# Keeping two row blocks on chip, pairing the row work and ordering the weight gradients by hand in an adaLN block's backward kernel

## The chip, the cores and the metric

One core of a Trainium2 chip. The metric is the device time of one execution in microseconds (us), median over the runs of a kernel. A comparison of times below uses fast runs only, and unless said otherwise of kernels that ran on the same chip in the same rounds. Single profiles are compared by stretch, with the granted clock beside them (1.00 is full speed of TensorE's clock). PE is TensorE, DVE VectorE, ACT ScalarE, POOL GpSimd; SP issues the transfers, SPq is its queue. "Fill" is matmul work without a fixed place, put where TensorE would wait.

## The reference

```python
def _fwd(A_x, A_w_r, A_w_i, B_w1, B_b1, B_w2, B_b2, c, w_mod):   # S=2048, D=512, F=1792, bf16
    sa, ca, ga, sb, cb, gb = (silu(c) @ w_mod) in six rows of 512
    h = layernorm(x) * (1 + ca) + sa
    x = x + ga * irfft2(rfft2(h) * (w_r + 1j * w_i))           # spectral branch
    h = layernorm(x) * (1 + cb) + sb
    x = x + gb * (relu(h @ w1 + b1) ** 2 @ w2 + b2)            # squared-ReLU MLP
    return x
_out, _vjp = jax.vjp(_fwd, ...); _grads = _vjp(grad_out)       # ... the output and nine gradients
```

## The kernel before

Transforms are GEMMs. The order of work: generated tables and the forward spectral stages (the gradient of h, `gT x w2T`, fills TensorE's holes: its 512-column results are evicted to `gab`), the forward rows, the FFN in four blocks of four rows, backward spectral stages, backward rows, with the gradients of w1 and w2 as fill. A scheduler orders each engine's instructions by priority; `LATE` means "only if nothing else is ready". The parts that the change touches:

```python
def rstd(nc, dst, var, K):                                    # GpSimd, two instructions
    nc.gpsimd.tensor_scalar(dst, var, 1e-5, None, op0=ALU.add)
    nc.gpsimd.tensor_tensor(dst, dst, K["nhalf"][...], op=ALU.pow)

def stage_g(b):                                               # forward rows, one at a time
    ...
        psY = spec_g23(tc, K, CS, t, rows, psR, psR)          # 4 psT matmuls, Tsb on ACT, 1 psY matmul
        nc.scalar.copy(out=yb[:, j, :], in_=psY)
        nc.vector.tensor_tensor(yg, yb[:, j, :], modb[:, GA_B, :], op=ALU.mult)
        nc.vector.tensor_tensor(xb[:, j, :], yg, xb[:, j, :], op=ALU.add)
        nc.vector.bn_stats(st, xb[:, j, :]); nc.vector.bn_aggr(mv, st)
        rstd(nc, inv2[:, t:t + 1], mv[:, 1:2], K)
        nc.vector.tensor_scalar(n2rows[:, hf + j, :], xb[:, j, :], mv[:, 0:1], inv2[:, t:t + 1], ...)
        nc.gpsimd.tensor_tensor(xb[:, j, :], xb[:, j, :], gbb2, op=ALU.add)      # bias b2
    nc.sync.dma_start(y_dram[...], yb); ...; nc.sync.dma_start(x1_dram[...], xb)
    ...
# backward spectral stages: all loads first, stores when a step is done
for gi in range(8):
    ...LF, Z (w_r), Z (w_i), X of group gi are loaded; n2_sb after gi == 1...
nc.sync.dma_start(K["LG"], LG_dram); nc.sync.dma_start(K["LGx"], LGx_dram)
def ew_b(gi, G):
    cmul(nc, ew, Z[gi], G, ...)
    gW = ew.tile([P, 2, 2, FP], BF16, name="gW")              # two buffers
    cmul(nc, ew, Xt[gi], G, gW...)
    nc.sync.dma_start(out2_view[...], gW...); nc.sync.dma_start(out3_view[...], gW...)
with Priority(tc, LATE):
    ...for fb in range(NFB): grad_w1(fb)                      # 16 units of 16 matmuls, then w2's 14
```

The order of the FFN stages g, t, h, o, gn of the four blocks is the same in both kernels.

## Time and profile before

The median was 585.62 us of 3 runs (583.81 to 588.2) when the prediction was made. The stretches of the profiled run (579.1 us), cut where TensorE starts another kind of work; the first inverse transform is the short one with `psG` matmuls:

| stretch | begins with | us | PE idle, us |
|---|---|---|---|
| start | launch | 98.6 | not used |
| inverse transform | first psG | 14.2 | 0 |
| C, forward rows | end of psG | 55.5 | 10.2 |
| D, FFN | first hidden-layer matmul | 189.5 | 18.2 |
| E, backward | first backward psB | 221.3 | 37.7 |

A stretch tells more than the whole: PE is busy 84% of the span, but C, E's first 54 us and the end lose for three different reasons. The lines themselves are in the prediction.

### The profile page before, as it was taken

What the parts mean: (1) busy time and instruction counts of PE and PEld (TensorE: products, weight loads), DVE (VectorE), ACT (ScalarE), POOL (GpSimd) and SP (SyncE); (2) the same over time, 40 slices, a digit from 0 to 9 for tenths busy, and PEclk for the clock granted to TensorE, in tenths of its full rate; (3) what the DMA queues carried; (4) which work ended last, traced back from release to release, by engine and by line L of the source; (5) the groups of instructions that cost most, each with busy time, mean ns of one, the idle gap of its engine ahead of it and who ended that gap; (6) DMA issues with size and microseconds to landing.
All of it is one profiled execution on the core that took longest, in us unless ns stands there. A gap on an engine that the chain in (4) does not pass through costs nothing. (4 is left out here: it accounts for less than half of the span.)

```text
span 579.1 us, 8005 instructions
## 1 busy us (share of the span) xinstructions
PE 486.9 (84%) x2670; PEld 239.3 (41%) x2710; DVE 386.6 (67%) x1016; ACT 241.8 (42%) x418; POOL 51.9 (9%) x130
## 2 busy tenths in 40 slices
PE   1767999987889898997889969895799978977977
PEld 0523467833334343443444423462563333433423
DVE  6897978378739679388348545362987999564531
ACT  3656754354535234243252412560267633244210
POOL 4233000046200004004000000000000000000000
PEclk9989999999999998999989989798899997999989
DMA  8958723467449329955954997897559953249991
GB/s 289 250 214 234 254 64 86 161 191 218 164 127 291 128 80 274 247 200 163 241 171 152 257 191 162 274 249 229 113 138 283 234 161 102 65 120 258 255 230 52
DMA packets 157409, 109.64 MB, mean 189 GB/s; under 512 B 87090, under 2 KB 144312, under 8 KB 156600
## 3 DMA queue, kind: packets, MB, share of 16 engines
q1 hardware_dynamic: 157368, 109.13, 68.0%
q8 instruction: 21, 0.34, 0.2%
q14 instruction: 20, 0.16, 0.1%
HBM read 43.22 MB, written 45.44 MB: 153 GB/s over the span
## 5 line engine op out<-in xcount | busy, mean ns | idle before, releaser
L646 PE MATMUL mm<-gT,w2T 128*128 128x512 bf16 x218 | 54.7, 379 | 16.2 <-DVE gab L649 10.5
L838 PE MATMUL og<-w,h 128*128 128x512 bf16 x219 | 55.9, 399 | 2.8 <-DVE h L781 1.8
L773 PE MATMUL mm<-h2T,w 128*128 128x512 bf16 x216 | 53.9, 386 | 2.4 <-ACT r L775 1.5
L1004 PE MATMUL mm<-g_sb,hn 128*128 128x512 bf16 x219 | 51.0, 388 | 3.9 <-DVE gw L1007 2.9
L775 ACT ACTIVATE r<-mm,b1col 128x512 bf16<-128x512 f32 x56 | 38.3, 688 | 38.0 <-PE mm L773 18.9
L941 PE MATMUL mm<-gab,n_sb 128*128 128x448 bf16 x256 | 53.1, 361 | 1.1 <-ACT gb1bc L934 0.6
L810 PE MATMUL og<-w1T,gab 128*128 128x512 bf16 x220 | 49.8, 379 | 0.3
L646 PEld LDWEIGHTS <-w2T 128*128 128x128 bf16 x224 | 21.5, 97 | 45.6 <-issue 16.7
L941 PEld LDWEIGHTS <-n_sb 128*128 128x128 bf16 x256 | 24.9, 99 | 27.3 <-issue 6.5
L1004 PEld LDWEIGHTS <-hn 128*128 128x128 bf16 x224 | 21.8, 99 | 32.4 <-issue 8.4
L773 PEld LDWEIGHTS <-w 128*128 128x128 bf16 x224 | 21.2, 98 | 32.9 <-issue 14.0
L838 PEld LDWEIGHTS <-h 128*128 128x128 bf16 x224 | 21.7, 102 | 28.3 <-issue 4.8
L394 PE MATMUL psT<-Cf,utcs 128*128 128x512 bf16 x123 | 32.5, 379 | 0.2
L810 PEld LDWEIGHTS <-gab 128*128 128x128 bf16 x224 | 21.5, 98 | 26.2 <-issue 1.5
L777 DVE TENSOR_TENSOR gab<-r,gab 128x512 bf16<-128x512 bf16 x56 | 27.1, 483 | 7.7 <-ACT r L775 7.1
L458 DVE SCALAR_TENSOR_TENSOR gm_junk<-wmc,onef,gmbc 128x512 bf16<-128x512 bf16 x24 | 18.0, 750 | 19.0 <-DMA wmc<-in_w_mod_dram 18.6
L812 ACT ACTIVATE cb<-og,inv 128x512 bf16<-128x512 f32 x16 | 10.9, 686 | 45.3 <-PE og L810 29.2
L742 POOL TENSOR_TENSOR xb<-xb,gbb 128x512 bf16<-128x512 bf16 x16 | 19.4, 1215 | 106.0 <-DVE n2rows L741 106.0
L649 DVE CAST gab<-mm 128x512 bf16<-128x512 f32 x28 | 19.2, 686 | 13.0 <-PE mm L646 13.0
L379 PEld LDWEIGHTS <-Z 128*128 128x128 bf16 x256 | 25.1, 98 | 6.3 <-DVE gW L415 1.7
L341 PE MATMUL psC<-AE,LFb 128*128 128x257 bf16 x120 | 17.1, 297 | 8.7 <-ACT G L343 8.6
L781 DVE TENSOR_TENSOR h<-r 128x512 bf16<-128x512 bf16 x56 | 23.2, 415 | 0.0
(282 smaller groups left out, 851.8 us busy)
## 6 DMA issues: line engine op xcount, KB each, us to landing
gh_dram<-gab SPq DMA_DIRECT2D x28, 256.0 KB, 3.2
h_dram<-h SPq DMA_DIRECT2D x28, 256.0 KB, 2.9
w<-in_B_w_dram SPq DMA_DIRECT2D x2, 1792.0 KB
wm<-in_w_mod_dram SPq DMA_DIRECT2D x3, 1024.0 KB, 11.7
wmc<-in_w_mod_dram SPq DMA_DIRECT2D x6, 512.0 KB, 5.3
out_dram<-gwm SPq DMA_DIRECT2D x6, 512.0 KB, 4.4
Z<-in_A_w_r_dram SPq DMA_DIRECT2D x16, 128.5 KB, 3.0
Z<-in_A_w_i_dram SPq DMA_DIRECT2D x16, 128.5 KB, 5.0
```

The lines of the kernel that those rows point to most:

```text
L379: nc.tensor.matmul(ps[:, ch, :], lhsT=Z[gi][:, x, ri, f0:f0 + P], rhs=lg_window(K, g, e + ri), start=(n == 0), stop=(n == 3))
L394: nc.tensor.matmul(ps, lhsT=CS[:, t, c].rearrange("p r a b -> p (r a b)"), rhs=K["Cf"][:, c, :], start=(c == 0), stop=(c == 3))
L646: nc.tensor.matmul(ps, lhsT=w2T[:, dc, fc * P:(fc + 1) * P], rhs=gT[b][:, dc, :], start=(dc == 0), stop=(dc == 3))
L742: nc.gpsimd.tensor_tensor(xb[:, j, :], xb[:, j, :], gbb2, op=ALU.add)
L773: nc.tensor.matmul(ps, lhsT=w1[:, dc, fc * P:(fc + 1) * P], rhs=h2T[b][:, dc, :], start=(dc == 0), stop=(dc == 3))
L775: nc.scalar.activation(r, ps, AF.Relu, bias=b1col[:, fc:fc + 1])
L777: nc.vector.tensor_tensor(gh, r, gh, op=ALU.mult)
L781: nc.vector.tensor_tensor(hT[b, fc], r, r, op=ALU.mult)
L810: nc.tensor.matmul(ps, lhsT=gaT[b][:, fc, j * P:(j + 1) * P], rhs=w1T[:, fc, :], start=(fc == 0), stop=(fc == NFC - 1))
L838: nc.tensor.matmul(ps, lhsT=hT[b, fc][:, j * P:(j + 1) * P], rhs=w2[:, fc, :], start=(fc == 0), stop=(fc == NFC - 1))
L941: nc.tensor.matmul(ps[:, 0:W4], lhsT=n2_sb[:, t, dc * P:(dc + 1) * P], rhs=ghn[t // 4][:, t % 4, fs], start=(t == 0), stop=(t == NT - 1))
L1004: nc.tensor.matmul(ps, lhsT=hn[:, t, :], rhs=g_sb[:, t, :], start=(t == 0), stop=(t == NT - 1))
```

## The change

Its intent: take the statistics' chain off GpSimd, halve the number of small row instructions, save 8 MB of round trips, and place each gradient GEMM by hand where another engine or a transfer would leave TensorE idle. The core of the diff (cuts marked):

```diff
+def rstd_act(nc, dst, var, K):
+    nc.scalar.activation(dst, var, AF.Sqrt, bias=K["eps"])
+    nc.vector.reciprocal(dst, dst)
 ...
+    AEs = make_ae(nc, lfp)            # was inside spec_f23: zeroed padding column of the AE tiles
 ...
-                nc.sync.dma_start(y_dram[:, ts, :], yb)
-                nc.sync.dma_start(x1_dram[:, ts, :], xb)
+            x1b[b] = rows.tile([P, TB, D], BF16, name="x1")
+            yb[b] = rows.tile([P, TB, D], BF16, name="y")
+            for j in range(0, TB, 2):            # pairs of rows
+                nc.vector.tensor_tensor(yg, y, modb[:, GA_B, None, :].broadcast_to([P, 2, D]), op=ALU.mult)
 ...
+                rstd_act(nc, inv2[:, t:t + 2], mv[:, :, 1], K)
-                    nc.gpsimd.tensor_tensor(xb[:, j, :], xb[:, j, :], gbb2, op=ALU.add)
 ... stage_o
+                    nc.tensor.matmul(ps, lhsT=K["ones_sq"][0:1, :], rhs=b2row, start=True, stop=False)
 ... backward spectral stages
-        for gi in range(8): ...all loads...
+        for gi in range(2):
+            load(gi)
-            gW = ew.tile([P, 2, 2, FP], BF16, name="gW")
+            gW = ew.tile([P, 2, 2, FP], BF16, name="gW", bufs=3)
+        def after_b(gi):
+            if gi + 2 < 8:
+                load(gi + 2)
+            if gi == 5: ...LG, LGx...
+            if gi > 0:
+                fill_w1(2)
-    with Priority(tc, LATE): ...grad_w1, grad_w2...
 ... last loop, per pair of rows
+            fill(t // 2)                          # one w1 or w2 unit
 ... GMod.emit: wmc and gwm in halves with bufs=4 instead of one whole buffer each
```

## The prediction

> **What bounds the kernel now.** I read the page's head first, then the busy time of each engine in eight stretches cut at the borders that the TensorE timeline shows, then TensorE's list of waits in the stretches with gaps, then the VectorE and TensorE timelines inside two of them. The head and the slices of the page:
>
> ```profile
> span 579.1 us, 8005 instructions
> PE 486.9 (84%) x2670; PEld 239.3 (41%) x2710; DVE 386.6 (67%) x1016; ACT 241.8 (42%) x418; POOL 51.9 (9%) x130
> PE   1767999987889898997889969895799978977977
> ```
>
> TensorE (PE) is the only engine near full. Its gaps lie in the first eighth, the fourth eighth and the last third. The stretches (columns: stretch, length, busy time of PE, weight load, DVE, ACT, POOL, granted clock, DMA share, GB/s):
>
> ```profile
> 113.50:167.00 53.50, 44.01 (x242) 19.72 (x245) 35.61 (x75) 26.11 (x47) 18.34 (x28) 1.00 0.52 163
> 167.00:357.00 190.00, 171.11 (x833) 74.53 (x849) 122.55 (x313) 69.35 (x108) 14.73 (x20) 0.96 0.73 200
> 357.00:411.00 54.00, 40.88 (x239) 23.69 (x241) 27.33 (x56) 19.11 (x36) 0.14 (x2) 0.84 0.82 232
> 428.00:511.00 83.00, 75.05 (x386) 32.25 (x387) 66.64 (x202) 39.78 (x83) 0.00 (x0) 0.96 0.59 167
> 511.00:579.00 68.00, 53.59 (x234) 22.80 (x238) 28.78 (x70) 18.73 (x32) 0.00 (x0) 0.97 0.80 191
> ```
>
> Call them C (forward row stage: x1, statistics, n2, filled with the first weight GEMM), D (the FFN), E1 (backward spectral stages), E2 (backward rows with the w1 gradient as fill) and E3 (w2 gradient alone). PE is idle 9.5 us in C, 19 in D, 13 in E1, 8 in E2, 14 in E3. TensorE's waits in C and in E1 name the two largest:
>
> ```profile
> PE mm L646 <- DVE gab L649: 9.0, 6, 2.6
> ...
> PE psC L341 <- ACT G L343: 8.6, 1, 8.6
> PE mm L930 <- DMA LFb<-LF_dram: 3.7, 1, 3.7
> ```
>
> In C, VectorE is late with an eviction because it sits, in order, behind rows whose rstd comes from GpSimd (VectorE timeline):
>
> ```profile
> 132.10 0.41 DVE L741 TENSOR_SCALAR n2rows<-xb,l_mv,inv 128x512 bf16<-128x512 bf16 x1 [0.77 <-POOL inv L405]
> 132.43 0.69 DVE L737 BATCH_NORM_STATS2 l_st<-xb 128x6 f32<-128x512 bf16 x1
> 133.03 1.00 DVE L734 TENSOR_TENSOR yg<-yb,modb 128x512 bf16<-128x512 bf16 x1
> 133.95 0.17 DVE L739 BATCH_NORM_AGGREGATE l_mv<-l_st 128x2 f32<-128x6 f32 x1
> 134.06 0.43 DVE L735 TENSOR_TENSOR xb<-yg,xb 128x512 bf16<-128x512 bf16 x1
> 134.41 0.68 DVE L649 CAST gab<-mm 128x512 bf16<-128x512 f32 x1
> ```
>
> The reader is to see 0.77 us waited for GpSimd, and yg taking 1.00 us where it takes 0.42 elsewhere: GpSimd runs its x1+bias add (1.15 us) just then. The n2 writes start at 132.1, 135.2, 138.4, 141.5: 3.15 us a row. TensorE needs 1.95 us a row (psY starts at 129.6 and 131.6 where nothing waits). In E1 the 8.6 us gap is a transfer: the chain of waits has an output store of the weight gradient gW taking 10.70 us at 390.8, queued behind bulk loads; gW has two buffers, VectorE stops, then ACT, then PE. In E3 the chain of waits alternates between w2-gradient matmuls, gwm stores and 5 us loads of wmc, which has one buffer.
>
> [...] tensor_tensor in bf16 takes 0.42 us on 512 columns and 0.69 on 1028, so a pair saves 0.15 us. [...] Both loads of this trace take 1283 ns; the changed kernel has a third, at its first Sqrt, and none later. [...] after the 8.6 us gap, 16 psC matmuls took 3.60 us against 1.95, and E1's granted clock is 0.84.
>
> **The change, part by part.** A built version gives the instruction order per engine; what follows uses it.
>
> *Start, 0 to 98.6.* Nearly untouched. The small AE memset moves ahead of the iotas that delayed it (a 2.2 us PE wait), and the order interleaves the first spectral groups earlier. Gain 3 us, between 0 and 8, a choice.
>
> *C.* Out go the GpSimd rstd (0.36 + 0.57 us a row), its bias add and the 0.42-to-1.00 stretching; in come a Sqrt on ACT and a reciprocal, per pair. VectorE per pair of rows was 6.3 us; now 2 x 0.69 (yg, x1), 2 x 0.69 (statistics), 2 x 0.18, 2 x 0.41 (n2), some 0.7 for Sqrt and reciprocal, one eviction of 0.69: 5.3 us against PE's 3.9. Also, since x1, y and n2 are held as two blocks of four, only 9 psY rows and 12 psT groups come before the FFN instead of 16; the last 66 GEMM matmuls (14 us) hide the rows. PE work at the pace of 0.216 us for 512 columns (56 w2-gradient matmuls in 12.48 us give 0.22): 114 x 0.216 + 48 x 0.216 + 9 x 0.216 + 1.5 = 38.4 us. With 3 us of stalls C is 41.5 instead of 53.5: gain 12.
>
> *D.* It receives the moved work, 16 psT + 7 psY = 5.0 us, and 16 new matmuls for the b2 row, 16 x 0.216 = 3.5 us. Pairing takes some 11 us off VectorE in the two products of the hidden layer (27.1 + 23.2 us in 112 instructions, about 39 in 56) and 5 in the row products; but VectorE is busy 64% here and not the bound. The y and x1 round trips through DRAM go (4 x 2 MB of 109.6 MB): they are hidden, only 2.5 us of PE waits in D name any load. Of the waits on n2rows, h, gx and gp (4.2 + 1.8 + 4.2 + 1.0) I let 3 us go; the n2 chain of the third block now has little filler after its last psY. Net loss 5.5 us.
>
> *E, 357 to 579, 222 us.* PE work by the paces of the timeline: spectral 13.8 + 13.9 + 13.7, w1 gradient 256 x 0.189 = 48.4, its bias sums 6, rows 17.3 + 5.1, w2 gradient 48.4: 166.7 us; over the mean granted clock of 0.96, 173.5. So 48 us is loss. Now two w1 units (6 us of PE) follow each spectral step: PE per step 10 us, VectorE 4 x 0.69 + 4 x 0.42 (4.0) + 2 x 2.0 = 8, so PE stays the bound; gW has three buffers, bulk LG loads come late, the next step's loads are spread. The 8.6 us gap and the slow clock behind it should go. In the row loop one GEMM unit per pair gives PE 6.3 us against VectorE's 4.5. In the tail wmc and gwm have four buffers. What stays: some 4 us at the start while Z and the 2 MB n2 load land (PE has 16 us of work before the first w1 unit); 3 us where n1 rows queue behind g (2 MB) and four transposed loads that cannot start before the LG space is free; 4 us in the tail; 3.5 us last eviction and store; 7 us of short gaps. 173.5 + 21.5 = 195: gain 27.
>
> Sum: 3 + 12 - 5.5 + 27 = 36.5 us, some 6%; 585.6 - 36.5 = 549, and I say 548.
>
> **Rivals.** (a) *A wait takes the place of the one removed*: TensorE's order is now fixed by hand, so a late load stops everything: the first w1 unit waits for n2, the first w2 units for g and hn, the rows for n1. For: n_sb took 10.6 us to land, hn 6.5, and the order puts four hn loads and g ahead of n1. Against: 12 to 16 us of PE work stands before each. With 6 to 8 us at each place, 565. (b) *VectorE becomes the bound* in the interleaved spectral steps: 8 of 10 us is close, and in-order gradient evictions sit inside the complex products. For: VectorE was busy 16.96 of 17 us at 411 to 428. It would cost about 1.5 us a step: 560. (c) *The transfers were hidden, and the x1/y part gives nothing*: this I believe of the DRAM part by itself; if the ACT Sqrt also just replaces the GpSimd wait, C gains only 5 us: 555. (d) *The gaps and the clock go together*: if E reaches 185 us and the clock stays near 1, 535.
>
> **Range and chances.** All rivals but a double failure leave more than 2% (under 574). PE work over the clock, plus the unavoidable start and end, is about 505, so under 525 is unlikely. Range 530 to 567. Faster by over 2%: 0.93; within: 0.05; slower: 0.02.
>
> **What would show it.** Right: PE's wait on gab gone from C, GpSimd near 20 us busy in all, the first hidden-layer matmul at about 150 us instead of 168; no gap over 3 us in the backward spectral steps, w1-gradient matmuls inside them and a clock above 0.95 there; DMA near 101 MB; the part from the first backward spectral matmul to the end near 195 us. Wrong: PE waits on n_sb, hn, g_sb or n1 of 5 us and more; VectorE above 90% in E1; ACT waiting for statistics before a Sqrt while Tsb is late; D longer than 200 us.

"Both loads of this trace" are the two table loads of ScalarE, at 0.73 and 10.66 us. The paces are the trace's: eight psB matmuls of 512 columns take 1.89 us with 0.38 for a single one, so (1.89 - 0.38) / 7 = 0.216 us each; thirteen of 448 columns take 2.62 with 0.35 for one, so 0.189. No trace stood behind the 0.7 us for Sqrt and reciprocal: that was the author's estimate. In the changed kernel it is 0.66 us from the end of the statistics (128.30) to the end of the reciprocal (128.96).

## The result, and the profile after

The changed kernel took 544.93 us (median of 4, 540.11 to 545.98) against 584.71 (median of 4, 578.83 to 588.2): the ratio is 0.9335, 95% interval 0.9236 to 0.9434. A ratio is the mean time of one kernel's fast runs over that of the other's fast runs of the same rounds, so not quite the ratio of the quoted medians. The prediction of 548 was 3 us off, in its range, and on the side it favoured.

The head and the slices of the page of the kernel after, to be held against those of before:

```profile
span 542.6 us, 7664 instructions
PE 483.9 (89%) x2684; PEld 237.9 (44%) x2726; DVE 362.5 (67%) x872; ACT 245.3 (45%) x427; POOL 16.5 (3%) x88
PE   0779899999987999999789997988999999789995
```

PE does the same work (483.9 against 486.9 us busy) in a span 36.5 us shorter. GpSimd fell from 51.9 to 16.5 us, VectorE by 24. The stretches C, D, E's spectral part, its rows and its end (columns as in the prediction: PE, weight load, DVE, ACT, POOL, clock, DMA share, GB/s):

```profile
108.30:150.40 42.10, 40.63 (x234) 18.72 (x238) 24.84 (x53) 21.84 (x40) 0.00 (x0) 1.00 0.24 77
150.40:347.10 196.70, 180.65 (x861) 78.05 (x876) 113.01 (x232) 78.28 (x125) 0.14 (x2) 0.95 0.66 178
347.10:424.40 77.30, 72.49 (x459) 39.47 (x462) 55.78 (x126) 27.70 (x51) 0.00 (x0) 0.98 0.70 207
445.40:511.00 65.60, 59.73 (x265) 23.88 (x269) 45.58 (x112) 37.96 (x77) 0.00 (x0) 0.95 0.98 253
511.00:542.60 31.60, 24.82 (x113) 10.27 (x112) 23.05 (x60) 10.91 (x21) 0.00 (x0) 0.96 0.90 240
```

C is all but full (1.5 us idle). D has 16 us idle and a clock of 0.95. In the rows the transfer engines are busy 98% of the time. VectorE's order in C, where before it waited 0.77 us for GpSimd in every second row and 0.17 us in the others:

```profile
126.16 0.73 DVE L748 TENSOR_SCALAR n2rows<-x,l_mv,inv 128x512 bf16<-128x512 bf16 x2
126.80 1.28 DVE L744 BATCH_NORM_STATS2 l_st<-x 128x6 f32<-128x512 bf16 x2
128.00 0.30 DVE L745 BATCH_NORM_AGGREGATE l_mv<-l_st 128x2 f32<-128x6 f32 x2
128.21 0.67 DVE L739 TENSOR_TENSOR yg<-y,modb 128x1024 bf16<-128x1024 bf16 x1
128.80 0.16 DVE L413 RECIPROCAL inv<-inv 128x2 f32<-128x2 f32 x1
128.91 0.69 DVE L740 TENSOR_TENSOR x<-yg,x 128x1024 bf16<-128x1024 bf16 x1
129.52 0.68 DVE L651 CAST gab<-mm 128x512 bf16<-128x512 f32 x1
130.12 0.73 DVE L748 TENSOR_SCALAR n2rows<-x,l_mv,inv 128x512 bf16<-128x512 bf16 x2
```

No line has a wait in brackets; the n2 writes of two pairs stand 3.96 us apart, where two single rows took 6.3. The next pair's yg is placed between one pair's statistics and its reciprocal, so the Sqrt's latency is covered: it runs on ScalarE from 128.33 to 128.62 us, and this reciprocal starts at 128.80. Of the four reciprocals in C the first and the last waited for it, 0.94 and 0.36 us.

| stretch | before | after | gain | predicted |
|---|---|---|---|---|
| start | 98.6 | 94.2 | 4.4 | 3 |
| inverse transform | 14.2 | 14.1 | 0.1 | 0 |
| C | 55.5 | 42.1 | 13.4 | 12 |
| D | 189.5 | 196.7 | -7.2 | -5.5 |
| E | 221.3 | 195.5 | 25.8 | 27 |
| span | 579.1 | 542.6 | 36.5 | 36.5 |

That the sum fits to the digit is luck: by medians the gain is 39.8 us, and the profile before is of the fastest run. Other profiles with the old code in E took longer there (b_nobias 223.5 us, b_ae 224.6, x_front 228.1; b_rstd's 230.7 is of a slow run), so against them E gained 28 to 33 us; those with the old start have their first psG at 98.9 to 101.0 us instead of 98.6. D, 187.4 to 190.7 us in all profiles with the old code there, does not depend on the choice. A sum that fits this well can also hide terms that are wrong in their reason. Twelve runs looked for them.

### The profile page after: what moved, and what is told of

The parts are those of the page before. It is cut to its first block, busy times and chain, and to the rows that moved or that the text cites. A ratio compares the mean times of both kernels' runs of the same rounds, so it can differ in the third digit from the quotient of the medians.

```text
span 542.6 us, 7664 instructions
## 1 busy us (share of the span) xinstructions
PE 483.9 (89%) x2684; PEld 237.9 (44%) x2726; DVE 362.5 (67%) x872; ACT 245.3 (45%) x427; POOL 16.5 (3%) x88
## 2 busy tenths in 40 slices
DMA packets 142094, 101.11 MB, mean 186 GB/s; under 512 B 86242, under 2 KB 129000, under 8 KB 141288
## 3 DMA queue, kind: packets, MB, share of 16 engines
HBM read 38.90 MB, written 41.25 MB: 148 GB/s over the span
## 5 line engine op out<-in xcount | busy, mean ns | idle before, releaser
L839 PE MATMUL og<-w,h 128*128 128x512 bf16 x218 | 57.5, 407 | 3.7 <-DVE h L784 2.9
L944 PE MATMUL mm<-gab,n_sb 128*128 128x448 bf16 x256 | 51.9, 361 | 3.1 <-DMA n_sb<-n_dram 3.1
L817 DVE SCALAR_TENSOR_TENSOR jk<-cb,onef,n2rows 128x512 bf16<-128x512 bf16 x16 | 12.0, 749 | 28.0 <-ACT cb L814 28.0
L400 ACT ACTIVATE Tsb<-psT 128x512 bf16<-128x512 f32 x32 | 19.0, 596 | 23.4 <-PE psT L397 23.0
L651 DVE CAST gab<-mm 128x512 bf16<-128x512 f32 x28 | 19.2, 685 | 14.2 <-PE mm L648 14.2
L782 DVE TENSOR_TENSOR gab<-r,gab 128x1024 bf16<-128x1024 bf16 x28 | 19.3, 689 | 10.6 <-ACT r L780 10.6
L840 ACT CAST o<-og 128x512 bf16<-128x512 f32 x16 | 9.2, 587 | 34.6 <-PE og L839 34.6
L653 ACT CAST gab<-mm 128x512 bf16<-128x512 f32 x28 | 16.3, 581 | 15.6 <-PE mm L648 15.6
```

Source lines behind the costliest of these rows:

```text
L651: nc.vector.tensor_copy(out=gaT[b][:, fc, :], in_=ps)
L782: nc.vector.tensor_tensor(gh, r, gh, op=ALU.mult)
L839: nc.tensor.matmul(ps, lhsT=hT[b, fc][:, (j + i) * P:(j + i + 1) * P], rhs=w2[:, fc, :], start=False, stop=(fc == NFC - 1))
L944: nc.tensor.matmul(ps[:, 0:W4], lhsT=n2_sb[:, t, dc * P:(dc + 1) * P], rhs=ghn[t // 4][:, t % 4, fs], start=(t == 0), stop=(t == NT - 1))
```

## The experiments

"First psB to second psG" below is the stretch in which the backward spectral steps run, up to the inverse transform.

### 1 and 2. The two halves: x_front and x_tail

The kernel is cut at the end of the FFN. x_front is the changed code before the cut and the old code after it; x_tail is the other way round (only names and the shape of one row adapted, and the X store padded, as the other half needs).

> The changed kernel up to the end of the FFN, the old code from the backward spectral stages to the end. Theory (the two halves add up, E is worth 26 us and the front 10): 585 - 10 = 575 us, ratio to before 0.983. Rival 1 (the front sets up the tail: early ghn loads, n2 stored whole, so part of E's gain comes with the front): 565 or less, ratio 0.966. Rival 2 (the front is worth nothing in time because the old tail waits for the same loads): 584, ratio 1.00.

> The old code up to the end of the FFN, the changed code from the backward spectral stages to the end. Theory: 585 - 26 = 559 us, ratio 0.956; no PE gap over 4 us in the spectral steps. Rival 1 (part of E's gain needs the front): 568 or more, ratio 0.97. Together with the other hybrid the two gains should add up to the whole change's 40 us within 6.

Measured on one chip with before at 587.57: x_front 573.1 (ratio 0.9751, interval 0.9686 to 0.9815), x_tail 557.46 (0.9488, 0.9421 to 0.9556). The gains are 14.5 and 30.1 us, 44.6 together where the whole change gave 39.8 by its medians: they add up within the 6 us asked for, so neither half needs the other within that error. In x_tail the first hidden-layer matmul still comes at 170 us and the stretch from first psB to second psG is 78.4 us, as in the changed kernel. In x_front the old gap is there again (PE waits 11.3 us for G). So two thirds of the change are behind the FFN.

### 3 and 4. The forward rows: b_rstd and b_nobias

Both are the kernel before with one of the two things that left GpSimd.

```diff
 b_rstd
-  rstd(nc, inv2[:, t:t + 1], mv[:, 1:2], K)
+  rstd_act(nc, inv2[:, t:t + 1], mv[:, 1:2], K)
 b_nobias
-  nc.gpsimd.tensor_tensor(xb[:, j, :], xb[:, j, :], gbb2, op=ALU.add)      (and the making of gbb2)
+  nc.tensor.matmul(ps, lhsT=K["ones_sq"][0:1, :], rhs=b2row, start=True, stop=False)   (stage_o)
```

> Kernel before with one edit: rstd of the second layernorm by a Sqrt on ScalarE and a reciprocal on VectorE, row by row; the x1+bias add stays on GpSimd, the rows stay single. Theory (VectorE's in-order wait for GpSimd's rstd makes evictions late): the 9.0 us of PE waits on gab in the forward row stage fall below 4, total 579 us, ratio 0.99. Rival 1 [...]: waits stay at 7 to 9 us, ratio 1.00. Rival 2 (ScalarE becomes late with Tsb, which is the same stall by another name): waits on Tsb of 4 us and more take their place.

> Kernel before with one edit: the GpSimd add of the bias to x1 goes, the bias enters stage o by a K=1 matmul as in the changed kernel; rstd stays on GpSimd. Theory (the add only stretches VectorE a little: 16 x 0.6 us of yg): waits on gab fall by 2 of 9 us, 16 new matmuls cost 3.5 us in the FFN, total 586 us, ratio 1.00. Rival [...]: waits on gab fall below 3 us, yg takes 0.42 us, and total 581 us, ratio 0.993.

What the runs show is the stretching itself, yg at 1.00 us beside GpSimd's add and 0.42 without, and the rivals are that this makes VectorE late.

PE's waits in C of b_rstd, then VectorE's waits in C of b_nobias (columns: engine, instruction, what it waited for, us in total, times, longest):

```profile
PE psY L399 <- ACT Tsb L397: 3.6, 5, 1.5
PE pst L760 <- DVE h2T L763: 0.6, 1, 0.6
```

```profile
DVE gab L646 <- PE mm L643: 7.8, 9, 1.1
DVE n2rows L740 <- POOL inv L405: 6.3, 8, 0.9
```

With Sqrt on ScalarE the 9.0 us of waits on gab are 0.5, and waits of 3.6 us on Tsb come up: ScalarE, now in the chain, is late in five places. C falls from 55.5 to 50.9 us. With the bias add gone and rstd still on GpSimd, VectorE waits for rstd as before (6.3 us in 8 rows, 5.7 before) and PE on gab 6.3 us; C stays at 55.4 us, as 2.4 us more of the fill GEMM fell into it (PE busy 47.7 instead of 45.3). yg, which took up to 1.00 us before, takes 0.39 to 0.43 in all 16 rows, so GpSimd's add did stretch it (by what mechanism was not shown). The theories hold: without the in-order wait for rstd 8.5 of the 9.0 us go, without the bias add 2.7; the two shares overlap. In times, b_rstd cannot be judged: three of its four runs counted as slow (583.9 us median, the one fast run 574.0), the profiled one among them; the granted clock in C was 1.00 all the same, as in the kernel before. Of the remaining 8.8 us between 50.9 and the changed kernel's 42.1, 4.9 are moved work (PE is busy 40.6 us in C instead of 45.5, since two blocks of four rows need only 9 psY before the FFN) and 3.3 the waits on Tsb, of which 0.3 us are left there.

b_nobias took less time all the same, 577.8 us, ratio 0.9836 (0.9768 to 0.9905; whether it is more than 2% is unclear), which no theory had. Its trace shows most of it in the start: the first psG came at 91.2 us instead of 98.6. The edit was not clean: with GpSimd's order changed, the zeroing of the AE tiles (their padding column) stood at 12.22 us, in the kernel before at 57.15. That led to the next experiment.

### 5. The start: b_ae

GpSimd's order in the kernel before, and the TensorE matmul that waits for its last line; then the same two in the changed kernel (columns: start, length, engine and line, operation, tiles, in brackets the idle time before it and what ended it):

```profile
56.65 0.55 POOL L138 IOTA cf_dr<- 128x512 int32 x1
57.15 0.14 POOL L332 MEMSET AE<- 128x2 bf16 x2
57.31 0.60 PE L341 MATMUL psC<-AE,LF 128*128 128x257 bf16 x4 [2.21 <-POOL AE L332]
```

```profile
1.30 0.14 POOL L327 MEMSET AE<- 128x2 bf16 x2
40.57 0.27 PE L343 MATMUL psC<-AE,LF 128*128 128x257 bf16 x1
```

A zeroing of 0.14 us stands behind every table that GpSimd generates, and these wait for VectorE (6.77 us before 53.47, 5.67 before 41.16). The page counts 2.2 us of PE waiting, because PE spent some 12 us before it on fill. b_ae is the kernel before with only this moved:

```diff
-        AEs = [aep.tile([P, 2, 514], BF16, name=f"AE{i}") for i in range(2)]     (in spec_f23)
-        for ae in AEs: nc.gpsimd.memset(ae[:, :, 256:257], 0.0)
+    AEs = make_ae(nc, lfp)                                                       (first thing, and from cdp for the way back)
```

> Kernel before with one edit: the AE tiles of the forward and backward spectral stages are allocated and their padding column zeroed early, as in the changed kernel, so that the zeroing no longer stands at the end of GpSimd's order. Theory (the start's gain comes from this alone): the first forward psC starts near 41 us instead of 57, the first psG at 91 to 94 instead of 98.6, the wait of 2.2 us on GpSimd is gone, total 5 us under before, ratio 0.991. Rival (PE only does its fill GEMM later): first psG earlier but the forward row stage longer by the same amount, ratio 1.00.

Ratio 0.9874 (0.9822 to 0.9926), 582.72 against 589.29. The first psC now starts at 41.25 us, the first psG at 92.9, but C grew to 59.0, because more fill was left for it (PE is busy 51.1 us there instead of 45.3): the first hidden-layer matmul comes 2.2 us earlier and the first backward psB 2.9. So theory and rival are both half right: some 5.7 us were gained at the start and 3.5 given back in C. The rest of the measured 6.6 us is not explained; that the profile before is of a fast run will be part of it.

### 6, 7 and 8. The gap in the backward spectral stages: b_gw3, b_lglate, b_loads

The prediction said that the 8.6 us gap was a store queued behind bulk loads, with gW's two buffers too few. The kernel before with each of the changed kernel's three remedies alone:

```diff
 b_gw3
+            gW = ew.tile([P, 2, 2, FP], BF16, name="gW", bufs=3)
 b_lglate
         spec_f23(..., ew_b)
+        nc.sync.dma_start(K["LG"], LG_dram); nc.sync.dma_start(K["LGx"], LGx_dram)      (were ahead of it)
 b_loads
-        for gi in range(8): ...loads...
+        for gi in range(2): load(gi)
+            if gi + 2 < 8: load(gi + 2)                  (in ew_b, after the two stores; LG at gi == 5)
```

> Kernel before with one edit: the tile gW of the backward spectral stages gets three buffers instead of two. Theory (the 8.6 us gap comes from VectorE waiting for a gW buffer whose store is queued behind bulk loads): the gap on G falls below 2 us, the stretch from the first backward psB to the second psG falls from 54 to about 46 us, total 8 us under before, ratio 0.986. Rival (the queue of transfers is the limit, not the buffer): a gap of 5 us or more appears at the next load or the next store, the stretch stays above 51 us, ratio 1.00.

> Kernel before with one edit: the two bulk loads of the inverse transform's tables (LG, LGx) are issued after the spectral loop instead of before it; two gW buffers stay. Theory (the store that held the gap waited behind these loads): the gap on G falls below 3 us, the stretch falls to about 47 us, and psG waits for LG under 2 us; ratio 0.986. Rival 1: psG waits 4 us and more for LG, ratio 1.00. Rival 2: the gap stays because Z, LF and X loads are queued there too, ratio 1.00.

> Kernel before with one edit: in the backward spectral stages only two groups are loaded ahead, each further group's loads are issued after the step's gW stores, LG at step 5, as in the changed kernel; two gW buffers stay. Theory (the single in-order transfer queue held the first gW store behind the loads of all eight groups, so neither a third buffer nor moving LG alone helped): first gW store issued within 3 us of its data instead of 12, gap on G under 3 us, the stretch from first psB to second psG 46 us instead of 54, total 8 us under before, ratio 0.986. Rival (bandwidth: 232 GB/s in that stretch is all there is): gaps of 5 us and more at loads, stretch above 51 us, ratio 1.00.

None of them was shown to be faster: ratios 1.0043 (0.9979 to 1.0106), 0.999 (0.9842 to 1.0139) and 1.0032 (0.9962 to 1.0102). The stretch from first psB to second psG took 52.1, 54.3 and 56.8 us, against 54.1. In b_gw3 VectorE's wait for a gW buffer was still 14.4 us (15.7 before) and PE's gap, 9.7 us, had only moved on to the first psG. The transfer queue of the kernel before shows why a third buffer changes little (all of these are issued by SP, one after the other):

```profile
387.38 1.72 SPq L962 DMA_DIRECT2D Z<-in_A_w_i_dram  x1
389.15 0.47 SPq L967 DMA_DIRECT2D LGb<-LG_dram  x1
389.66 0.43 SPq L968 DMA_DIRECT2D LGxb<-LGx_dram  x1
390.13 0.62 SPq L974 DMA_DIRECT2D out_dram<-gW  x1
390.80 0.76 SPq L975 DMA_DIRECT2D out_dram<-gW  x1
```

The first gW store is issued only when the loads of nearly all groups have been. b_loads mends just that: its first store is issued at 377.66 instead of 390.13, and no wait for a gW buffer is left on VectorE. Yet PE then waits 5.9 us for LF and 5.4 us for LGx. The stretches of before, b_loads and, from the next experiment, a_nofill:

```profile
357.80:411.90 54.10, 40.09 (x235) 23.56 (x236) 28.23 (x58) 19.50 (x37) 0.14 (x2) 0.84 0.82 232
```

```profile
360.10:416.90 56.80, 41.35 (x235) 23.51 (x236) 35.57 (x72) 19.77 (x37) 0.14 (x2) 0.87 0.94 233
```

```profile
343.10:394.90 51.80, 39.90 (x252) 23.55 (x250) 34.84 (x70) 20.70 (x39) 0.00 (x0) 0.93 0.86 251
```

Whatever the order, some 12.5 to 13 MB (54.1 us x 232 GB/s; 51.8 x 251) have to pass while PE has only 40 us of work, and the transfer engines are busy 82 to 94% of the time. b_loads' rival named this. In b_loads the wait only went from a store to a load. How much of the stretch is bandwidth is not shown: share times length is 44 us of transfer time in before (0.82 x 54.1) and in a_nofill (0.86 x 51.8), 53 in b_loads, more than PE's 40 but up to 10 us below the stretch. The rest can lie in the order of loads and stores in the one queue, and no run moved fewer bytes.

### 9. The interleave: a_nofill

```diff
-            if gi > 0:
-                fill_w1(2)
 ... after spec_f23
+    fill_w1(14)
```

> Changed kernel with one edit: the fourteen w1-gradient units run in one piece after the spectral loop instead of two per step; buffers and loads as changed. Theory (the interleave fills PE while VectorE does the complex products): the steps then go at VectorE's pace of 5 to 6 us against 4 of PE, so the stretch from first psB to second psG grows from 77 to about 90 us, total 557 us, ratio 0.953. Rival (three gW buffers and late loads did it all): stretch 80 us, total 548, ratio 0.938.

551.92 us, ratio 0.9475 (0.9409 to 0.954); a_dram (below), the changed kernel but for its traffic, had 0.936 in the same rounds, so the edit cost about 1.2% or 6 to 7 us. With three gW buffers and loads step by step, but without the units, PE again waits 5.0 us for G, 3.4 for LGx and 3.1 for LF, and the stretch is the 51.8 us of the line above. Behind the wait for G stands a transfer too: VectorE waits 4.8 us for a load of Z just before. From first psB to the end of the inverse transform, with all fourteen units in it, it is 109.8 us, and in the changed kernel 98.3, so in its own part of the kernel the edit cost 11.5 us; D, whose code is unchanged, was 4.3 us shorter in this profile, with a few matmuls in another order. The number lay between theory and rival: the theory had the reason wrong (VectorE's pace; once the loads are there, VectorE takes 3.8 us a step, as in the kernel before from 371.91 to 375.70) and its size too large. What the units hide is the waits for transfers.

### 10. The round trips: a_dram

```diff
 stage_g
+            nc.sync.dma_start(y_dram[:, TB * b:TB * b + TB, :], yb[b])
+            nc.sync.dma_start(x1_dram[:, TB * b:TB * b + TB, :], x1b[b])
 stage_gn, stage_o
+            nc.sync.dma_start(yb[b], y_dram[...])
+            nc.sync.dma_start(x1b[b], x1_dram[...])
```

> Changed kernel with the round trips put back: each block of four rows of y and x1 is stored to DRAM after the forward row stage and loaded again into the same tile before its use in the FFN stage, 8 MB more traffic (109 MB). Theory (hidden): ratio to the changed kernel's own 0.93 to before stays, 0.93 to 0.94; FFN stretch 197 us within 3. Rival (the DRAM part carries the gain): FFN stretch longer by 6 us and more, waits on x1 or y of 2 us and more each, ratio 0.945 to 0.96.

546.08 us, ratio 0.936 (0.9284 to 0.9436) against the changed kernel's 0.9335; D is 198.7 us. The 8 MB (109.50 MB against 101.11) were hidden, as the theory said. The blocks stay on chip in this run; what holding them is worth in C's order was not tested alone.

### 11. The stalls that are left: imp1

The changed kernel with five edits. In D: the scaling of w1T is placed after the first hidden stage, and the last readers of a grad_out block are emitted inside the next hidden stage, where its load is issued as well. In E: n2 is loaded in four pieces, the first two n1 pairs are queued ahead of the transposed hn loads, gw has six buffers and one GMod moves into the row loop.

```diff
+                if fc == 4: late.flush()                          (stage_h)
+                if fc == 8: load_g(b)
-        for fc in range(NFC): ...w1T scaling...                   (ahead of the rows)
         stage_h(0)
         stage_t(1)
+        for fc in range(NFC): ...w1T scaling...
-        nc.sync.dma_start(n2_sb, n2_dram)
+        for b in range(NB): nc.sync.dma_start(n2_sb[:, TB * b:TB * b + TB, :], n2_dram[...])
+        load_rows(0); load_rows(2)                                (ahead of load_hn; n1, gxl bufs=3)
-        gw ... bufs=3 / n % 2 == 1
+        gw ... bufs=6 / n in (2, 3, 5, 7)
```

> Changed kernel with five edits at the stalls that its trace still shows: w1T scaling after the first hidden stage (2.9 us wait on h), gb's last readers flushed inside the hidden stage and its load issued there (3.2), n2 loaded in four blocks (3.1), n1 and gx1 rows of the first two pairs queued ahead of the transposed loads (3.7), six gw buffers and one GMod moved into the row loop (3.0 at the end). Theory (each is a wait at the head of an in-order queue, and the slow clock after it goes too): 12 us of the 16 and some 3 us of slow clock go, total 531 us, ratio to before 0.912. Rival (transfers are at 0.95 of their engines' time in the last 100 us, so waits there only move): 6 us, 539, ratio 0.924.

525.72 us, ratio 0.8893 (0.8832 to 0.8954); against the changed kernel, measured in other rounds, that is 0.8893 / 0.9335 = 0.953. It is better than the theory, and only in part for its reason. By the profiles the gain is all in D. The lines of D in the changed kernel that prompted the first edit (VectorE, then TensorE):

```profile
163.32 0.69 DVE L782 TENSOR_TENSOR gab<-r,gab 128x1024 bf16<-128x1024 bf16 x1 [0.79 <-ACT r L780]
164.75 0.76 DVE L720 TENSOR_TENSOR w1T<-w1T,modb 128x512 bf16<-128x512 bf16 x2 [0.73 <-DMA w1T<-in_B_w_dram]
165.43 0.61 DVE L721 TENSOR_SCALAR w1T<-w1T,nmean 128x512 bf16<-128x512 bf16 x2
```

```profile
173.87 1.16 PE L839 MATMUL og<-w,h 128*128 128x512 bf16 x4 [2.86 <-DVE h L784]
174.82 1.06 PE L779 MATMUL mm<-h2T,w 128*128 128x512 bf16 x2
175.67 1.06 PE L839 MATMUL og<-w,h 128*128 128x512 bf16 x2
```

28 scaling instructions take VectorE from 164.75 to 173, while h (its next product, needed by TensorE) waits its turn; PE stops for 2.86 us. Then two matmuls take 0.85 us from start to start (174.82 to 175.67) where the fourteen of one og tile take 3.13 from 339.97 to 343.10: 0.43 us each instead of 0.22. The slow stretch lasts about 3 us. The slow clock of D stands behind pauses: 0.60 from 173.8 to 178 us, 0.53 and 0.50 from 270 to 278 behind and between pauses of up to 1.60 us, 0.50 from 328.8 to 332 behind one of 3.24. D in imp1:

```profile
149.50:327.40 177.90, 172.47 (x859) 75.38 (x873) 114.26 (x232) 76.95 (x125) 0.14 (x2) 0.99 0.76 197
```

D is 18.8 us shorter with the same matmuls: idle time fell from 16.1 to 5.4 us and busy time, at a clock of 0.99 instead of 0.95, from 180.7 to 172.5. So pauses and slow clock went together, 10.7 and 8.2 us. The two edits also let the scheduler order the blocks differently (the first gn stage before the second hidden stage), and the small waits of the changed kernel around 266 to 275 us are gone; how the 18.8 us divide among these was not tested.

In E the rival was right. From first psB to the end it took 193.2 us in the changed kernel and 192.6 in imp1 (both to PE's last matmul); the wait on n2 is still 3.9 us and those on q, for n1, 5.7 us:

```profile
PE acc L1101 <- DVE q L1098: 5.7, 3, 3.1
PE mm L948 <- DMA n_sb<-n_dram: 3.9, 1, 3.9
```

### 12. The bias: imp2

imp1 with the K=1 matmuls of the bias undone in another way.

```diff
-                    nc.tensor.matmul(ps, lhsT=K["ones_sq"][0:1, :], rhs=b2row, start=True, stop=False)
-                    nc.scalar.copy(out=o[:, i, :], in_=ps)
+                    nc.vector.tensor_tensor(o[:, i, :], ps, b2bc, op=ALU.add)
```

> The five-edit kernel with one edit more: the bias b2 is added by VectorE as it evicts the output of the second layer (128x512 from PSUM, 0.69 us each), instead of by 16 K=1 matmuls, and ScalarE's 16 copies of 0.59 us go. Theory (the 16 matmuls lie on TensorE's path, 0.32 us apart in the trace): the FFN stretch falls from 178 to 174 us or less, total 522 us, ratio to before 0.882. Rival (VectorE, in order behind row products, evicts late): waits on the PSUM tile og of 4 us and more, FFN stretch 178 us or more, ratio 0.89.

517.42 us (median of 6, 516.82 to 519.74), ratio 0.88 (0.876 to 0.8839). D:

```profile
149.60:320.10 170.50, 166.26 (x860) 74.16 (x858) 124.09 (x248) 68.19 (x109) 0.14 (x2) 1.00 0.76 206
```

D fell by 7.4 us, twice the theory; PE waits for an eviction of og only 0.2 us. 16 x 0.32 us (one matmul's start to the next's, at 339.65 and 343.10 us of the changed kernel; others take 0.22, and why was not shown) is 5.1 us of it. The rest was not separated; the clock is at 1.00 and there are fewer waits. Against the changed kernel, over before as the common measure, this is 0.88 / 0.9335 = 0.943.

## Why the prediction was right, point by point

- **C** (12 predicted, 13.4 measured; 41.5 us long predicted, 42.1 measured): right in size and reason. The first hidden-layer matmul came at 150.4 us ("about 150"), the wait on gab is gone. The term for VectorE was too dear: 5.3 us a pair in the sum, 3.96 in the trace, since the Sqrt's latency, for which 0.7 us was put in, is covered, and instructions overlap at their ends (n2 ends at 126.89 us, the statistics start at 126.80). As PE was the bound at either pace, it cost nothing. b_rstd showed that rstd is behind 8.5 of the 9.0 us of waits, and b_nobias that the bias add, to which the prediction gave a share, is behind 2.7.
- **Start** (3, measured 4.4): the right instruction, sized by the wrong number. The 2.2 us PE wait is what is left after fill; the spectral chain gained 16.7 us at its first psC. b_ae showed 5.7 us at the first psG, of which 3.5 are given back in C as fill that moved there. The prediction's "Gain 3" holds as the net.
- **D** (-5.5, measured -7.2): the moved work was near its size (16 psT 4.3 us and 7 psY 2.6 us busy, 6.9 against 5.0; busy counts each group to its end, and the next can start before that: in the lines of experiment 11 one ends at 175.03 us, 173.87 + 1.16, and the next starts at 174.82), the b2 row wasn't: "16 x 0.216 = 3.5" is 16 x 0.32 = 5.1 us by the starts in the trace, and 7.4 us were gained when it went. The credit "I let 3 us go" failed: the waits on n2rows did fall (4.2 to 0.5), but h waits rose from 1.8 to 2.9, and gaps in the rows' part came up. What the prediction did not see at all is that the D it planned held nearly 19 us of pauses and slow clock that two edits could take away; it treated D as a stretch with little to win.
- **E** (27, measured 25.8, or 28 to 33 against the other profiles): right in size, wrong in one reason. The step that failed is "an output store ... queued behind bulk loads; gW has two buffers", with its remedy "gW has three buffers, bulk LG loads come late, the next step's loads are spread". Three buffers, late LG and step-wise loads each gave nothing alone, and the last two with three buffers but without the units (a_nofill) still left waits of 11.5 us. The transfers take some 44 of the 54 us (share times length); the fourteen w1 units, 48.4 x 14/16 = 42 us of PE work, are what turned the stretch from transfers to PE (72.5 busy of 77.3 us, clock 0.98, no gap over 3.1). "PE stays the bound" was the right half of the sentence; its sum for VectorE ("4 x 0.69 + 4 x 0.42 (4.0)") is 4.4 as written, while the products take 3.8 us a step by a_nofill's trace. The interleave is worth 6 to 7 us of the whole time and 11.5 us in its own part of E; how the others divide among the earlier loads of the last gh block, the padded X transfers, pairs, GMod's halves and the order of the tail was not tested.
- **Rivals.** (a) came in small: 3.1 us on n2, and 3.65 us at the first n1 row (5.5 in all four waits on q; this row's load was issued at 461.32 us, behind three transposing loads of hn that held the queue for 13.14 us, where a plain load took 0.4 to 0.6), where 6 to 8 each were feared. (b) did not come: VectorE is busy 55.8 of 77.3 us. (c)'s first half is shown by a_dram: the DRAM part gives nothing by itself. Its second half did not come: PE's wait on Tsb in C is 0.3 us. (d) was half there: E stayed at 195.5 us, but the clock did follow the gaps, as imp1 then used.
- **What would show it**: GpSimd 16.5 us ("near 20"), 101.11 MB ("near 101"), D 196.7 us, just under the 200 of the wrong side; the third table load is there, from 118.11 to 119.39 us with the Sqrt at 119.40, and no other.

## What to carry to other kernels

Before giving a buffer to a queued store, multiply the stretch's length by the transfer engines' busy share: if that is more than TensorE's own work there, as here (44 us against 40), look for work of another kind to put beside it. A small wait in a page can stand for a long delay that fill has covered: here the page counted 2.2 us, and in b_ae, without it, the first psC came 16.1 us earlier. Pauses of TensorE can cost more than their length: here 10.7 us of them went together with 8.2 us of slow clock. After a change that fits its prediction, ask each stretch's sum for its reasons anyway: here the best next gain (D from 196.7 to 170.5 us) lay in the stretch that the change had made slower.
